# Decode attention block with gated MLP on one core: the loads of x move to GpSimd's queue, the query weights come first on ScalarE's, and ten tiny loads of x are added to SP's

## Chip, cores and metric

The kernel runs on one core of a Trainium2 chip. The metric is the device time of one launch in microseconds (us), as the median of several runs. Before the change it is 193.39 us (three runs, 193.19 to 193.43).

## What is computed

One token x of 512 bf16 numbers passes a layer norm. The result goes through attention over 32 heads with a cached window of 4096 keys and values of 128 numbers each, and beside it through a small MLP whose output gates the attention's.

```python
xn = _layernorm(x)
W = min(4096, max(256, Sk // 4))                    # 4096 of 32768
q = (xn @ wq).reshape(1, 1, 32, 128).transpose(0, 2, 1, 3)
k, v = k_cache[:, :, Sk - W:, :], v_cache[:, :, Sk - W:, :]
p = softmax(einsum("bhqd,bhkd->bhqk", q, k) * 128 ** -0.5)
s = einsum("bhqk,bhkd->bhqd", p, v).transpose(0, 2, 1, 3).reshape(1, 1, 4096) @ wo
hs = concat(shifted quarters of gelu(_layernorm(xn) @ w1)) @ w2   # one token: all quarters are zero
x1 = xn + hs
g = silu(x1 + gelu(_layernorm(x1) @ w3) @ w4)
return x + s * g
```

The two caches' windows are 33.6 MB each, wq and wo 4.2 MB each, w2, w3 and w4 together 3.3 MB. The profile counts 79.02 MB moved.

## The kernel before

**Tiling.** The 32 heads go in eight groups of four (G = 4). A group's keys are one tile K0 to K7 of 128 partitions by 128 rows by 128 numbers (4096 KB), its values one tile V0 to V7 of the same size. VectorE (DVE) works out the scores of the first 64 or 80 rows of a K tile in four parts, each a product with the query (L321) and a sum (L323); TensorE (PE) turns the other rows (L339), ScalarE (ACT) copies them out of PSUM (L342) and TensorE makes their scores (L350). The exponentials are ScalarE's (L388), the products with V TensorE's (L427). Values run two groups behind keys (LAG = 2).

**Buffers.** K tiles share three buffers (K_BUFS = 3); the first part of the output weights, wo_24, takes one of their turns between K5 and K6. V tiles share two (V_BUFS = 2). The V pool lies where the weights wq, w2, w3 and w4 lay, so V0 waits until these have landed and been used. A K or V load therefore waits for the engines to be done with the tile that had its buffer.

**The head of the kernel.** x is loaded twice, as x_bf (L79: 128 partitions, 8 bytes each) and as x_row (L82: four rows of 256 bytes), both from ScalarE's queue, ahead of the query weights wq (L84: 4096 KB, 32 KB to a partition). SP's queue issues, in this order, w2 (512 KB), w3 (1376 KB), w4 in two pieces (1280 and 96 KB), and then K0 in two halves, K0a and K0b, K1 and K2. x_bf feeds the first layer norm: L183, L160 to L178, then xn (L186, L188) and, through L194 and L196, the operand of the query product. TensorE's order is written by the scheduler: norm of x, the product of w2 with zeros (L233), L194, norm of x1, the product with w3 (a_ps, L252), and only then the 32 query products with wq (L208). The queries are spread to all partitions by L214 and L216 (q_bc), and q_bc and K0a are what the first L321 waits for. x_row is used in L242 and at the very end in L653.

**SP's queue** holds all other loads. Their order is the program's (`keep_in_program_order`), and a load that waits holds up all behind it. In each step s of the main loop (L531) K of group s is issued first (L534), then V of group s - 2 (L541, L545), then, in steps 5 and 7, parts of wo (L549, L551, L552): blocks of 2048, 1024 and 512 KB, here called wo_24, wo1 and wo2. The last V tile is issued in three pieces, V7a (2048 KB), V7b and V7c (1024 KB each), then two loads of wo_rows (256 KB each) and the output.

**Completion semaphores.** The loads issued by SP and ScalarE take eight completion semaphores in turn; the program makes a load wait until the load that had its semaphore before has landed. In what follows such a semaphore is a lane. The kernel before uses them so, each row in order of time:

| lane | loads |
|---|---|
| 0 | x_bf, K0b, K5, wo2 |
| 1 | w2, K1, V3, V6 |
| 2 | x_row, K2, wo_24, V7a |
| 3 | wq, V0, K6, V7b |
| 4 | w3, K3, V4, V7c |
| 5 | w4 (1280 KB), V1, K7, first wo_rows |
| 6 | w4 (96 KB), K4, V5, second wo_rows |
| 7 | K0a, V2, wo1, output |

So K0b waits for x_bf and K2 for x_row.

Of the kernel before, what the change touches and what calls it, by code (L numbers as in the profile page):

```python
# [8 lines left out]
P = 128  # L9
BF16 = mybir.dt.bfloat16  # L10
# [16 lines left out]
def kernel(  # L27
# [14 lines left out]
    nc = tc.nc  # L42
# [11 lines left out]
    KC = D // P  # L54
# [9 lines left out]
    small = ctx.enter_context(tc.tile_pool(name="small", bufs=1))  # L64
# [10 lines left out]
    def load(dst, src):  # L75
        return tc.keep_in_program_order(nc.sync.dma_start(out=dst, in_=src))  # L76

    x_bf = small.tile([P, KC], BF16, name="x_bf")
    nc.scalar.dma_start(out=x_bf[:], in_=A_x.rearrange("a b (p c) -> p (a b c)", p=P))  # L79
    x_row = small.tile([P, P], BF16, name="x_row")  # L80
    nc.gpsimd.memset(x_row[:], 0.0)
    nc.scalar.dma_start(out=x_row[0:P:32, :], in_=A_x.rearrange("a b (j n) -> (a b j) n", j=KC))  # L82
    wq_sb = wts.tile([P, KC, HD], BF16, name="wq_sb")
    nc.scalar.dma_start(out=wq_sb[:].rearrange("p c n -> p (c n)"),  # L84
                        in_=A_wq.rearrange("(a b c) n -> b a (c n)", a=4, c=KC))
# [5 lines left out]
    load(w4_sb[:, 0:10, :], B_w4[0:10 * P, :].rearrange("(p c) n -> p c n", p=P))  # L91
    load(w4_sb[0:96, 10, :], B_w4[10 * P:F, :])


    def load_kv(pool, cache, g, cuts=(0, CP)):
        t = pool.tile([P, CP, Dh], BF16, tag="kv", name="kv")
        src = cache[0, G * g:G * g + G, W0:, :].rearrange("a (b c) d -> b a (c d)", b=PB)
        dst = t[:].rearrange("p c d -> p (c d)")
        for c0, c1 in zip(cuts, cuts[1:]):
            load(dst[:, c0 * Dh:c1 * Dh], src[:, :, c0 * Dh:c1 * Dh])  # L100
        return t
# [115 lines left out]
    for b in range(2):  # L217
# [5 lines left out]
        for t in range(2):  # L223
            rows = slice(64 * t, 64 * t + 64)
            nc.scalar.copy(out=q_pair[rows, 4 * b:4 * b + 4, :, G * t:G * t + G].rearrange("p g l a -> p g a l"),
                           in_=qt_ps[rows].bitcast(BF16).rearrange("p g (a m l) -> p g a m l", a=G, l=2)[:, :, :, 0, :])
# [38 lines left out]
    for i in range(11):  # L265
        n = P if i < 10 else 96
# [44 lines left out]
    def k_open(g):  # L311
        st[g] = {
            "sT": ps_s.tile([P, CP - 64, G], FP32, tag="sT", name="sT"),
            "S": sm_pool.tile([P, CP], FP32, tag="S", name="S"),
        }

    def k_vector(g, kn, part):
        m = nd(g) // 4
        rows = slice(m * part, m * part + m)
        prod = prod_pool.tile([P, 20, Dh], BF16, tag="prod", name="prod")  # L320
        nc.vector.tensor_tensor(out=prod[:, 0:m, :], in0=kn[:, rows, :],  # L321
                                in1=q_bc[:, g:g + 1, :].to_broadcast([P, m, Dh]), op=ALU.mult)
        nc.vector.tensor_reduce(out=st[g]["S"][:, rows], in_=prod[:, 0:m, :], axis=AX.X, op=ALU.add)  # L323
# [3 lines left out]
    def batches(g):  # L327
        n, m = nd(g), CP - nd(g)
        k = -(-m // 8)
        edges = [n + 2 * (m // 2 * i // k) for i in range(k + 1)]  # L330
        return list(zip(edges, edges[1:]))

    def k_turn(g, kn, b):
        c0, c1 = batches(g)[b]
        n = (c1 - c0) // 2
        pt = ps_tr.tile([P, 4, P], FP32, tag="pt", name="pt")
        for i in range(n):
            c = c0 + 2 * i
            nc.tensor.transpose(pt[:, i, :], kn[:, c:c + 2, :].rearrange("p c d -> p (c d)").bitcast(FP32),  # L339
                                ident_f[:])  # L340
        kts[b] = kt_pool.tile([P, 4, 2 * P], BF16, tag="kt", name="kt")
        nc.scalar.copy(out=kts[b][:, 0:n, :], in_=pt[:, 0:n, :].bitcast(BF16))  # L342

    def k_scores(g, b):
        kt = kts.pop(b)
        c0, c1 = batches(g)[b]
        for i in range((c1 - c0) // 2):
            c = c0 + 2 * i - nd(g)
            for l in range(2):
                nc.tensor.matmul(st[g]["sT"][:, c:c + 2, :].rearrange("p c a -> p (c a)"),  # L350
                                 lhsT=kt[:, i, l::2], rhs=q_pair[:, g, l, :], start=(l == 0), stop=(l == 1))
# [55 lines left out]
    def load_wo(i):  # L407
        h0, n = blocks[i]
        load(wo_blk[i], A_wo[h0 * P:(h0 + n) * P, :].rearrange("(p t) n -> p t n", p=P))
# [4 lines left out]
    def load_rows(h, n):  # L414
        load(wo_rows[:, h - h_part:h - h_part + n, :],
             A_wo[h * P:(h + n) * P, :].rearrange("(h p) n -> p h n", p=P))
# [93 lines left out]
    def y_open():  # L510
        yr[0] = ps_tr.tile([P, KC, P], FP32, tag="pt", name="yr_ps")
        zeros(yr[0][:])
# [12 lines left out]
    NG = H // G  # L525
# [5 lines left out]
    for s in range(NG + LAG):  # L531
        h = s - LAG
        last = h == NG - 1
        kn = load_kv(k_pool, A_k_cache, s, (0, 64, CP) if s == 0 else (0, CP)) if s < NG else None  # L534
        if s == LAG:
            wts_guard.__exit__(None, None, None)
            v_pool = ctx.enter_context(tc.tile_pool(name="v", bufs=V_BUFS))
            wo_blk[2] = v_pool.tile([P, 4, D], BF16, tag="wo_4", bufs=1, name="wo_4")
            wo_rows = v_pool.tile([P, H - h_part, D], BF16, tag="wo_rows", bufs=1, name="wo_rows")
        if last:  # L540
            v = load_kv(v_pool, A_v_cache, h, cuts)  # L541
            for r in (H - G, H - 2):
                load_rows(r, 2)
        elif h >= 0:
            v = load_kv(v_pool, A_v_cache, h)  # L545
        if h == 3:
            wo_24 = k_pool.tile([P, 32, D], BF16, tag="kv", name="wo_24")
            wo_blk[0], wo_blk[1] = wo_24[:, 0:16, :], wo_24[:, 16:24, :]
            load_wo(0)  # L549
        if h == 5:  # L550
            load_wo(1)  # L551
            load_wo(2)  # L552

        if s < NG:
            nb = len(batches(s))

            def keys(b0, b1):
                for b in range(b0, b1):
                    k_turn(s, kn, b)
                    if b > 0:  # L560
                        k_scores(s, b - 1)

            k_open(s)
            k_vector(s, kn, 0)
            keys(0, 2)
            if s == 7:
                v_turn(h - 1)
                v_add(h - 1)
                v_out(h - 1)
            elif s > 1:  # L570
                sm_den(s - 2)
                sm_rden(s - 2)
            elif s == 1:
                sm_max(0)
            k_vector(s, kn, 1)
            keys(2, 4)
            if s == 7:
                sm_den(h)
                sm_rden(h)
                keys(4, nb - 2)  # L580
                sm_turn(s - 1)
                keys(nb - 2, nb)
            else:
                if s > 0:
                    sm_turn(s - 1)
                keys(4, nb)
            k_scores(s, nb - 1)
            sm_own(s)
            if s == 7:
                k_vector(s, kn, 2)  # L590
                v_wide(h, v)
                sm_exp(s - 1)
                v_turn(h)
                y_open()
                k_vector(s, kn, 3)
                v_add(h)
                v_out(h)
                ox_spread(1)
                sm_max(s)
                continue  # L600
            if s > 0:
                sm_exp(s - 1)
            if h > 0:
                v_turn(h - 1)
            k_vector(s, kn, 2)
            if h >= 0:
                v_wide(h, v)
            if h > 0:
                v_add(h - 1)
                v_out(h - 1)  # L610
            if s == 6:
                ox_spread(0)
            k_vector(s, kn, 3)
            if s == 6:
                ox_pick(0)
            if s > 0:
                sm_max(s)
        elif s == NG:
            ox_pick(1)
            sm_turn(NG - 1)  # L620
            sm_exp(NG - 1)
            y_wide(1, False)
            sm_den(NG - 2)
            sm_rden(NG - 2)
            y_wide(0, False)
            warm(3)
            v_wide(h, v)
            sm_den(NG - 1)
            sm_rden(NG - 1)
            v_turn(h)  # L630
            v_add(h)
            v_out(h)
            ox_spread(2)
        else:
            v_open(h)
            warm(3)
            v_wide(h, v, cuts[1], last=False)
            ox_pick(2)
            y_wide(2, True)
            nc.scalar.copy(out=y_sum[:], in_=yr[0][:].rearrange("p j n -> p (j n)"))  # L640
            v_wide(h, v, cuts[2], cuts[1])
            v_turn(h)
            v_add(h)
            rows_add(y_ps, ind, y_sum, False)
            v_part(h, v, cuts[2], CP)
            v_out(h)
            for r in range(H - G, H):
                y_head(r)
# [36 lines left out]
```

## Time and profile before

| | |
|---|---|
| median of three runs | 193.39 us (193.19 to 193.43) |
| span of the profiled execution, first to last instruction | 191.2 us |
| left over between the two | 2.2 us |
| DMA | 79.02 MB, mean 413 GB/s over the span |
| busy: DVE / PE / ACT / POOL | 150.9 / 116.4 / 89.2 / 2.3 us |
| x_bf: issued, landed | 0.74, 4.69 us |
| wq: issued, landed | 2.32, 19.87 us |
| K0a, K0b, K1 landed | 25.99, 32.09, 41.82 us |
| K6, V4, K7, V5 landed | 134.15, 143.80, 153.52, 163.17 us |
| wo1, wo2, V6 landed | 165.64, 166.86, 176.52 us |
| V7a, V7b, V7c, second wo_rows landed | 181.46, 183.89, 186.33, 187.61 us |

Times count from the span's start. A load has landed when its completion semaphore has received its last step, which is later than its last record. The trace also holds one record for each piece of a load that a DMA engine moved, with its queue, size and duration; q1 is SP's queue, q10 ScalarE's, q8 and q14 fetch instructions and tables. The 2.2 us between the span and the median lie outside what the profile shows.

### The profile page before, as it was taken

How to read it: one execution, taken by the hardware profiler on the slowest of the kernel's cores; microseconds unless marked ns; L12 is line 12 of the kernel's file. 1: busy time of each engine (PE TensorE's matmuls, PEld its weight loads, DVE VectorE, ACT ScalarE, POOL GpSimd, SP SyncE). 2: the span in 40 equal slices, each digit the busy share in tenths (PEclk: the TensorE clock that was granted, in tenths of full speed). 3: DMA queues.
4: the chain of work that ended last, by engine and by line, in shares of the span. 5: the costliest groups of instructions: out<-in, count | busy, mean ns of one | idle time of the engine just before them, and what ended most of it. 6: DMA issues, size and time to landing. Idle time of an engine off the chain costs nothing.

```text
span 191.2 us, 2839 instructions
## 1 busy us (share of the span) xinstructions
PE 116.4 (61%) x1159; PEld 74.2 (39%) x1159; DVE 150.9 (79%) x175; ACT 89.2 (47%) x191; POOL 2.3 (1%) x11
## 2 busy tenths in 40 slices
PE   1653754989825368256845772680888189739762
PEld 0430222767614334143334441540763077313322
DVE  1660159979999999999999999999999999980111
ACT  2001370888794076427464564542475148733120
POOL 2110000000000000000000000000000000000000
PEclk9999695555755557955695588557567858975998
DMA  6999999999999999999999999999999998999990
GB/s 211 447 430 404 431 418 439 439 439 437 432 434 439 432 429 432 432 439 432 422 432 432 418 422 418 452 439 435 439 432 434 435 432 372 471 425 405 420 371 32
DMA packets 4572, 79.02 MB, mean 413 GB/s; under 512 B 624, under 2 KB 1232, under 8 KB 1488
## 3 DMA queue, kind: packets, MB, share of 16 engines
q1 hardware_dynamic: 4264, 74.65, 91.6%
q10 hardware_dynamic: 296, 4.20, 5.1%
q8 instruction: 9, 0.15, 0.3%
q14 instruction: 3, 0.02, 0.0%
HBM read 78.84 MB, written 0.00 MB: 412 GB/s over the span
## 4 chain that ended last, share of the span: by engine, by line
DVE 46%; DMA 43%; PE 5%; ACT 3%; issue 1%; SPq 1%; ACTq 0%; DVEq 0%
DMA kv<-in_A_k_cache_dram 31%; DVE S L323 28%; DVE prod L321 15%; DMA kv<-in_A_v_cache_dram 10%; ACT kt L342 3%; DMA x_bf<-in_A_x_dram 2%; PE pt L339 2%; PE ov L427 1%; DVE m L366 1%; DVE S L364 1%; SPq L76 1%; PE sT L350 1%; DVE mx L374 1%; PE oT L461 1%; PE ot_ps L444 0%
## 5 line engine op out<-in xcount | busy, mean ns | idle before, releaser
L323 DVE TENSOR_REDUCE S<-prod 128x20 f32<-128x2560 bf16 (+1 forms) x32 | 86.0, 2686 | 1.1
L342 ACT COPY kt<-pt 128x1024 bf16<-128x1024 bf16 x52 | 51.2, 1013 | 40.4 <-PE pt L339 38.7
L339 PE MATMUL pt<-ident_f,kv 128*128 128x128 f32 x208 | 46.7, 376 | 10.8 <-DMA kv<-in_A_k_cache_dram 10.8
L321 DVE TENSOR_TENSOR prod<-kv,q_bc 128x2560 bf16<-128x2560 bf16 (+1 forms) x32 | 45.4, 1418 | 3.9 <-DMA kv<-in_A_k_cache_dram 3.7
L339 PEld LDWEIGHTS pt<-ident_f,kv 128*128 128x128 f32 x208 | 34.2, 196 | 14.4 <-DMA kv<-in_A_k_cache_dram 10.5
L350 PE MATMUL sT<-q_pair,kt 128*128 128x8 bf16 x416 | 19.4, 170 | 15.7 <-ACT kt L342 15.5
L350 PEld LDWEIGHTS <-kt 128*128 128x128 bf16 x416 | 16.4, 104 | 26.8 <-ACT kt L342 25.8
L427 PE MATMUL ov<-kv,pT 128*16 128x512 bf16 x248 | 22.0, 515 | 1.4 <-DMA kv<-in_A_v_cache_dram 1.4
L388 ACT ACTIVATE pT<-S,mb 128x128 bf16<-128x128 f32 x32 | 13.9, 573 | 0.3
L372 PE MATMUL mt_ps<-ident_f,m 128*1 128x128 f32 x8 | 2.9, 359 | 17.4 <-DVE rden L399 16.9
L433 ACT COPY ov_sb<-ov 128x512 f32<-128x512 f32 x8 | 4.7, 586 | 17.1 <-PE ov L427 17.1
L427 PEld LDWEIGHTS <-pT 128*16 128x16 bf16 x248 | 6.9, 109 | 13.2 <-issue 11.4
L359 ACT ACTIVATE own<-sT,par 128x48 f32<-128x48 f32 (+1 forms) x32 | 7.5, 356 | 3.7 <-PE sT L350 3.7
L444 PE MATMUL ot_ps<-ident_f,ov_sb 128*128 128x128 f32 x32 | 7.1, 359 | 2.9 <-ACT mb L384 1.9
L211 DVE CAST q_row<-qr_ps 128x512 bf16<-128x512 f32 x1 | 0.7, 692 | 9.9 <-PE qr_ps L208 9.9
L388 ACT ACTIVATION_READ_ACCUMULATOR pT<-S,mb 128x1 f32 x32 | 8.3, 258 | 0.0
L372 PEld LDWEIGHTS mt_ps<-ident_f,m 128*1 128x1 f32 x8 | 0.6, 80 | 17.9 <-DVE rden L399 17.2
L399 DVE RECIPROCAL rden<-den_ps 128x4 f32<-128x4 f32 x8 | 1.4, 175 | 7.0 <-PE den_ps L394 7.0
L381 PE MATMUL mb_ps<-md,par_t 5*128 5x4 f32 x16 | 3.9, 311 | 4.1 <-DVE md L376 4.1
L255 ACT ACTIVATE a_row<-a_ps 128x384 bf16<-128x384 f32 x1 | 0.5, 491 | 12.0 <-remote 12.0
L444 PEld LDWEIGHTS ot_ps<-ident_f,ov_sb 128*128 128x128 f32 x32 | 4.5, 178 | 3.9 <-ACT mb L384 2.3
L208 PE MATMUL qr_ps<-wq_sb,xq_bf 128*1 128x512 bf16 x32 | 3.1, 566 | 3.7 <-DMA wq_sb<-in_A_wq_dram 3.7
(122 smaller groups left out, 81.6 us busy)
## 6 DMA issues: line engine op xcount, KB each, us to landing
kv<-in_A_k_cache_dram SPq DMA_DIRECT2D x7, 4096.0 KB, 31.3
kv<-in_A_v_cache_dram SPq DMA_DIRECT2D x7, 4096.0 KB, 30.6
wq_sb<-in_A_wq_dram ACTq DMA_DIRECT2D x1, 4096.0 KB, 17.6
kv<-in_A_k_cache_dram SPq DMA_DIRECT2D x2, 2048.0 KB, 27.4
wo<-in_A_wo_dram SPq DMA_DIRECT2D x1, 2048.0 KB
kv<-in_A_v_cache_dram SPq DMA_DIRECT2D x1, 2048.0 KB
kv<-in_A_v_cache_dram SPq DMA_DIRECT2D x2, 1024.0 KB, 17.6
w_sb<-in_B_w_dram SPq DMA_DIRECT2D x1, 1376.0 KB, 9.1
```

The lines of the kernel that those rows point to most:

```text
L321: nc.vector.tensor_tensor(out=prod[:, 0:m, :], in0=kn[:, rows, :], in1=q_bc[:, g:g + 1, :].to_broadcast([P, m, Dh]), op=ALU.mult)
L323: nc.vector.tensor_reduce(out=st[g]["S"][:, rows], in_=prod[:, 0:m, :], axis=AX.X, op=ALU.add)
L339: nc.tensor.transpose(pt[:, i, :], kn[:, c:c + 2, :].rearrange("p c d -> p (c d)").bitcast(FP32), ident_f[:])
L342: nc.scalar.copy(out=kts[b][:, 0:n, :], in_=pt[:, 0:n, :].bitcast(BF16))
L350: nc.tensor.matmul(st[g]["sT"][:, c:c + 2, :].rearrange("p c a -> p (c a)"), lhsT=kt[:, i, l::2], rhs=q_pair[:, g, l, :], start=(l == 0), ...
L359: nc.scalar.mul(s["own"][:, 0:m, a], s["sT"][:, 0:m, a], par[:, a:a + 1])
L372: nc.tensor.transpose(mt_ps[:], s["m1"][:], ident_f[:])
L381: nc.tensor.matmul(mb_ps[:], lhsT=par_t[:].rearrange("k b a -> k (b a)"), rhs=md[:], start=True, stop=True)
L388: nc.scalar.activation(out=s["pT"][:, :, a], in_=s["S"][:], func=ACT.Exp, scale=scale, bias=mb[:, a:a + 1], accum_out=s["sum"][:, a:a + 1])
L427: nc.tensor.matmul(ov[r:r + 4 * G], lhsT=s["pT"][:, c:c + 4, :].rearrange("p i a -> p (i a)"), rhs=v[:, c:c + 4, :], start=(i < 4), stop=( ...
L433: nc.scalar.copy(out=s["ov_sb"][:], in_=ov[:])
L444: nc.tensor.transpose(ot_ps[:, step * j:step * j + P], s["ov_sb"][:, j, :], ident_f[:])
```

## The change

x_bf and x_row are issued by GpSimd, so that wq is the first load on ScalarE's queue. A small tile `marks` is added, into which SP loads ten tiny pieces of x (k rows of 32 bytes, k as listed; nothing reads them): five after K7 in step 7, and five after wo2 in the same step.

```diff
-    nc.scalar.dma_start(out=x_bf[:], in_=A_x.rearrange("a b (p c) -> p (a b c)", p=P))
+    nc.gpsimd.dma_start(out=x_bf[:], in_=A_x.rearrange("a b (p c) -> p (a b c)", p=P))
     x_row = small.tile([P, P], BF16, name="x_row")
     nc.gpsimd.memset(x_row[:], 0.0)
-    nc.scalar.dma_start(out=x_row[0:P:32, :], in_=A_x.rearrange("a b (j n) -> (a b j) n", j=KC))
+    nc.gpsimd.dma_start(out=x_row[0:P:32, :], in_=A_x.rearrange("a b (j n) -> (a b j) n", j=KC))
...
+    marks = small.tile([16, 16, 16], BF16, name="marks")
+
+    def mark(ks):
+        for k in ks:
+            load(marks[0:k, k, :], A_x[0, 0, 0:16 * k].rearrange("(k n) -> k n", k=k))
...
         kn = load_kv(k_pool, A_k_cache, s, (0, 64, CP) if s == 0 else (0, CP)) if s < NG else None
+        if s == NG - 1:
+            mark((1, 3, 5, 7, 2))
...
             load_wo(1)
             load_wo(2)
+            mark((9, 11, 13, 15, 14))
```

In the built program this moves more than the diff shows. GpSimd's loads have semaphores of their own, so the lanes of all later loads turn. The marks are called m1, m3 and so on by their k:

| lane | loads after the change |
|---|---|
| 0 | wq, K2, wo_24, m2, m14 |
| 1 | w2, V0, K6, V5, V6 |
| 2 | w3, K3, V4, wo1, V7a |
| 3 | w4 (1280 KB), V1, K7, wo2, V7b |
| 4 | w4 (96 KB), K4, m1, m9, V7c |
| 5 | K0a, V2, m3, m11, first wo_rows |
| 6 | K0b, K5, m5, m13, second wo_rows |
| 7 | K1, V3, m7, m15, output |

K0b and K1 no longer wait for a lane; K2 waits for wq; V5 waits for K6, wo1 for V4, wo2 for K7, and V6 for V5. GpSimd's order becomes: x_bf, the memsets of x_row and ident_bf, x_row, ident_bf's select, ident_f's memset, the power of the first norm (L178 before), and only then ident_f's select. On VectorE only the reduction that makes `ind` (L120 before) moves, two places later. TensorE's and ScalarE's orders are otherwise the same.

## Prediction

> **What bounds the kernel.** I read the DMA rows of the page first, then the chain, then what SP's queue waits for, then the timeline at the three places that the change touches: the head, the stretch from 130 to 168 us, and the tail.
>
> ```profile
> DMA  6999999999999999999999999999999998999990
> q1 hardware_dynamic: 4264, 74.65, 91.6%
> q10 hardware_dynamic: 296, 4.20, 5.1%
> q8 instruction: 9, 0.15, 0.3%
> DVE 46%; DMA 43%; PE 5%; ACT 3%; issue 1%; SPq 1%; ACTq 0%; DVEq 0%
> ```
>
> The queues' shares add to 97.0% of the span: 185.5 us on each of 16 engines. By the trace's records the first byte of a load moves at 1.74 us and the last load lands at 187.61, a stretch of 185.9 us. So the DMA engines have at most some 0.4 us without a record in the whole kernel. The bound is the sum of the records' durations; an earlier load gains only by starting the stream earlier, and a later one loses only by letting it run dry. The chain names DVE for 46%, since K buffers become free by DVE; but a buffer that comes free late costs nothing while other loads are queued. At 130.25 us, when K7 is issued, the engines are still at K6, landing at 134.15, and then V4, until 143.80: 13.5 us of stock. For V7a, issued at 166.55 with V6 landing at 176.52, it is 10.0 us.
>
> DVE is nearly a second bound, though:
>
> ```profile
> DVE prod L321 <- DMA kv<-in_A_k_cache_dram: 1.5, 2, 1.0
> DVE mx L374 <- PE mt_ps L372: 0.5, 2, 0.4
> ```
>
> These are all of DVE's waits from 41.9 to 172 us: 2.0 us, 1.0 of it ahead of K1 at 41.91. A delay that DVE has at 42 us is carried to the tail almost whole. And in the tail TensorE works just behind the landings:
>
> ```profile
> 181.50 1.04 PE L427 MATMUL ov<-kv,pT 128*16 128x512 bf16 x16 [1.02 <-DMA kv<-in_A_v_cache_dram]
> ...
> 183.93 0.61 PE L427 MATMUL ov<-kv,pT 128*16 128x512 bf16 x8 [0.41 <-DMA kv<-in_A_v_cache_dram]
> ...
> 186.38 0.96 PE L461 MATMUL oT<-pT,kv 128*128 128x4 bf16 x32 [0.17 <-DMA kv<-in_A_v_cache_dram]
> ```
>
> It waits 1.02 + 0.41 + 0.17 = 1.6 us for the three pieces of V7.
>
> **Part 1: wq first, SP's waits on x gone.** SP waits for x like this:
>
> ```profile
> SPq L76 <- DMA x_bf<-in_A_x_dram: 1.4, 1, 1.4
> SPq L76 <- DMA x_row<-in_A_x_dram: 0.9, 1, 0.9
> ```
>
> K0b and K2 are thereby issued at 4.71 and 6.83 us, while the engines have w2, w3, w4, wq and K0a to move until 26 us. Taking 2.3 us of such waiting away starts no byte earlier: gain 0. The new wait of K2 for wq holds it to some 14 us, with K0b and K1 (landed at 32.09 and 41.82) queued ahead of it: cost 0. The stream's start is w2's, issued at 0.73 us, and stays.
>
> What changes is the order in which the head's bytes come. In the records the two queues take turns piece by piece: x_bf's 8-byte records (9 ns) alternate one for one with w2's of 4096 bytes (159 ns), and later wq's eight records to an engine of 32 KB (1213 ns) with w3's of 11,008 (413 ns) and others. In the kernel before ScalarE's first records came at 2.35 us; wq, now first, takes its turns from there. Six of w2's eight are then left: 6 x (1.213 + 0.159) = 8.2, so w2 ends near 10.6 us (it landed at 4.52). The last two of wq alternate with w3: 2 x 1.63 = 3.3, so wq ends near 13.9 instead of 19.87, and w3, with six records left, near 16.4 instead of 10.32. The sum of bytes ahead of K0a is the same, so K0a still lands at 26.0.
>
> TensorE's order makes w3 count: a_ps (2.9 us, from 13.25 to 16.17) stands ahead of the query product, so it now starts near 16.5 and the query product near 19.4 instead of 19.91, when it waited for wq. Half a us earlier buys nothing, for DVE's first product waits for K0a:
>
> ```profile
> 26.09 1.23 DVE L321 TENSOR_TENSOR prod<-kv,q_bc 128x2048 bf16<-128x2048 bf16 x1 [2.19 <-DMA kv<-in_A_k_cache_dram]
> ```
>
> **Part 2: x through GpSimd.** No load of GpSimd's is in this trace. The row nearest to it is the same load from ScalarE, 0.74 to 4.69: 3.95 us. That is the low end. The high end is that GpSimd's records take turns singly as ScalarE's did, now against 32 KB records of wq in each round: eight rounds of 1.37 to 1.63 us from about 3 us on, so x_bf lands about when wq does, near 14.2 us.
>
> What x may cost is worked out back from K0a. From x's landing to z_bf is 13.20 - 4.69 = 8.5 us, a_ps 2.9, and from the query product to the first q_bc 24.02 - 19.91 = 4.1: x + 15.5 us, against 26.0. Up to x at 10.5 us nothing moves; with the 1.0 us that DVE waits ahead of K1, up to 11.5. I take the near row with a us or so on top, x at 5 to 6 us: cost 0. GpSimd's own order costs nothing either: ident_f's select (0.29 us) now follows the power (7.50 to 8.05), and `ind`, its first reader, was moved behind on DVE.
>
> The Trainium skill (DMA: Bandwidth & Descriptors, "Queues, rings and completion order" and "SWDGE vs HWDGE vs iDMA") says that an engine drains a whole packet of one ring before it turns to the next, and that GpSimd's descriptors are put into packets of up to 64. By that rule x_bf's eight pieces on an engine would need one turn, not eight, and x would land near the low end. The turns of single 8-byte records in this trace are of ScalarE's queue and neither bear it out nor speak against it.
>
> **Part 3: the ten marks.** As transfers: a mark is at most one data record and one semaphore record on an engine. Records of 8 bytes took 9 ns and of 256 bytes 15 to 18, semaphores 9, so a mark costs an engine 18 to 27 ns, and ten at most 0.27 us, if they all fall on the engine that ends last; nothing if they fall on others (the engines' last steps for V6 came between 174.60 and 176.52, so 15 of them have slack). I take 0.1.
>
> As issues on SP and by their lanes:
>
> ```profile
> 130.25 0.54 SPq L76 DMA_DIRECT2D kv<-in_A_k_cache_dram  x1
> 130.88 1.30 SPq L76 DMA_DIRECT2D kv<-in_A_v_cache_dram  x1
> 132.22 1.06 SPq L76 DMA_DIRECT2D wo<-in_A_wo_dram  x2
> 148.33 20.06 SPq L76 DMA_DIRECT2D kv<-in_A_v_cache_dram  x4
> ```
>
> After K7 at 130.25 come five marks, 0.4 to 0.55 us each as SP's other issues; the lanes that m7 and m2 wait for (V3, wo_24) had landed at 119.52 and 124.43. V5 waits for K6 and goes out at 134.2 instead of 130.88, with V4 and K7 queued until 153.5. wo1 waits for V4: 143.8. wo2 waits for K7: 153.5, with V5 queued until 163.17. The next five marks go out by 156. Then **V6 waits for V5**: 163.2 instead of 148.33. Queued behind V5 are then only wo1 and wo2, which end on the slowest engine at 166.86, 3.7 us on, and on the fastest at 164.95. From an issue to its first record w2 took 1.74 - 0.73 = 1.0 us, so V6's records come from 164.3: in time on all engines, with 0.6 us to spare on the fastest and 2.5 on the slowest. V7a waits for wo1 (165.64) and, as before, for TensorE (166.55); V7b for wo2 (166.86, it went out at 167.15); V7c and the rest for marks just behind wo2. Their stock is V6's 9.7 us. So the cover is thin in one place, and holds. TensorE needs V5 at 164.60, after it landed; V5, wo1, wo2 and V6 keep their places in the stream. Cost 0.
>
> **Sum.** The profiled execution: 191.2 us of span and 2.2 outside. Head 0, x 0, waits 0, marks +0.1: 191.3 and 2.2, or 193.5 us against the median of 193.39.
>
> **The rivals.**
> - **x lands late (slower).** With x at 14.2 us DVE starts K1 2.7 us late. It gets back the 0.55 us that it waits for K6 and up to 0.36 at L374, so it enters the tail some 2 us late; TensorE's 1.6 us of waits absorb most, but not all in one order (y_wide and the warm-ups stand between). I put the end 0.7 us later, 194.1; between 2.7 - 0.9 - 1.6 = 0.2 and, if only the wait of 1.02 us counts, 1.7. It decides from x at 11.5 us on. For it: the records' one-by-one turns. Against: the near row of 3.95 us, and x's issue at the same instant as wq's, whose queue gave its first record only at 2.35.
> - **V6 runs dry (slower).** If an issue takes longer than 3.7 us to its first record behind a deep queue, the slowest engine stands still; with 3.95 us, a small load's whole time, by 0.3 us, and the skew of 1.9 us between engines may add to it: 193.8 to 194.5. Against: w2's 1.0 us.
> - **A cheaper head (faster).** w2's 4096-byte records in the cold head took up to 849 ns; all 256 of that size took 198 ns in the mean against a usual 159, which is 0.6 us to an engine. If wq's large records, coming first, bear the start better, up to 0.6 us of it comes back: 192.9. Against: the slow records are the first of the stream, whatever they carry.
> - **The change does nothing where it matters:** that is my forecast.
>
> The Trainium skill (DMA: Bandwidth & Descriptors, "Issuing engines are not separate DMA queues") says the same of the head: loads from several engines run on the same 16 DMA engines and interleave, so another issuer saves only issue time. The trace agrees: SP's and ScalarE's records alternate on the same engines and the total rate stays near 430 GB/s.
>
> **How the numbers follow.** 0.2% of the time is 0.39 us, about what a measurement can tell from no change. Forecast (x before 11.5 us, V6 in time): 0.57. x late 0.24, V6 dry 0.07, cheaper head 0.12. Of the forecast's 0.57 I give 0.02 to more than 0.2% slower. The late x mostly ends past 193.78 us, but a fifth of it within: so slower 0.28, same 0.60, faster 0.12. The range runs from 192.9, the cheap head, to 194.6, within the late x.
>
> **What would show it.** Right: x_bf landing before 11 us, L321's first product at 26.1 with a wait for K0a, K1's first product at 41.9; wq landing near 14 and w3 near 16.5; V6 issued near 163.2 and landing at 176.5; V7c landing at 186.3. Wrong: a first product that starts when q_bc is written, DVE without waits at K1 and K6, or a slice near 164 us in which the DMA row drops below 9.

## The result, and the profile after

The changed kernel takes 194.29 us (median of 17 runs, 193.74 to 195.2), the kernel before on the same chip 193.41 (17 runs, 193.14 to 194.07): a ratio of 1.0047, interval 1.0036 to 1.0059. That is 0.9 us slower, where 0.1 us was forecast. The time lies within the range; the likeliest case, no difference that can be measured, did not come, and the range held by luck: it went up to 194.6 for an x that lands too late to be free, which did not happen.

The profiled execution took 193.82 us with a span of 191.7, so 2.1 us lie outside of it, as before (2.2): the loss is inside the span. The page's DMA rows and its chain, in the order in which they were shown of before:

```profile
DMA  6999999999999999999999999999999999999990
q1 hardware_dynamic: 4424, 74.65, 91.4%
q10 hardware_dynamic: 144, 4.19, 5.1%
q0 software_dynamic: 64, 0.00, 0.0%
DVE 46%; DMA 41%; PE 6%; ACT 3%; SPq 2%; issue 1%; ACTq 0%; DVEq 0%
```

q0 is GpSimd's queue, new here: 64 records without a visible share. The marks are 160 more records on q1. The row of tenths shows nothing; the loss is smaller than a slice can tell. Two of DVE's waits between 41 and 175 us (us in total, times, the longest), those that the prediction showed of before, are the same to 0.2 us, so nothing that x's detour did at the head has reached the main loop by way of DVE:

```profile
DVE prod L327 <- DMA kv<-in_A_k_cache_dram: 1.6, 2, 1.1
DVE mx L380 <- PE mt_ps L378: 0.6, 1, 0.6
```

At the head, the timeline has the cast that waits for x_bf, and the first product, which waits for K0a as before:

```profile
8.95 0.17 DVE L189 CAST x_f<-x_bf 128x4 f32<-128x4 bf16 x1 [7.61 <-DMA x_bf<-in_A_x_dram]
...
25.82 1.22 DVE L327 TENSOR_TENSOR prod<-kv,q_bc 128x2048 bf16<-128x2048 bf16 x1 [2.41 <-DMA kv<-in_A_k_cache_dram]
```

x_bf is 4.2 us later than before and this costs the first product nothing: it starts at 25.82, 0.27 us earlier than before, since K0a landed at 25.72 instead of 25.99. Up to wo2 the whole stream is 0.2 us ahead of before (K1 41.62, V5 162.97, wo2 166.68). Then it loses. SP's issues in that stretch (start, us to the next, with a wait inside where it is long):

```profile
130.64 1.74 SPq L76 DMA_DIRECT2D marks<-in_A_x_dram  x5
...
134.01 0.54 SPq L76 DMA_DIRECT2D kv<-in_A_v_cache_dram  x1
143.62 10.06 SPq L76 DMA_DIRECT2D wo<-in_A_wo_dram  x2
153.72 1.92 SPq L76 DMA_DIRECT2D marks<-in_A_x_dram  x5
163.04 6.92 SPq L76 DMA_DIRECT2D kv<-in_A_v_cache_dram  x4
```

V6 goes out at 163.04, when V5 has landed, 14.7 us later than before. One line for the stretch from 163 to 172 us (busy times of the engines, then TensorE's clock, DMA share, GB/s) of the kernel before and of the one after:

```profile
163.00:172.00 9.00, 4.62 (x60) 2.44 (x59) 8.21 (x13) 4.64 (x16) 0.00 (x0) 0.85 1.04 444
```

```profile
163.00:172.00 9.00, 5.89 (x59) 2.55 (x58) 8.31 (x13) 4.64 (x16) 0.00 (x0) 0.77 1.02 421
```

The last column is the finding: 23 GB/s less over 9 us are 0.21 MB, or 0.5 us at 444 GB/s, while the share of busy time hardly falls. Most of the loss is records that take longer; the table behind e4_twelve has them. The tail is late by what is left of this, with TensorE still just behind the landings:

```profile
181.92 1.04 PE L433 MATMUL ov<-kv,pT 128*16 128x512 bf16 x16 [0.45 <-DMA kv<-in_A_v_cache_dram]
...
184.35 0.61 PE L433 MATMUL ov<-kv,pT 128*16 128x512 bf16 x8 [0.40 <-DMA kv<-in_A_v_cache_dram]
...
186.80 0.96 PE L467 MATMUL oT<-pT,kv 128*128 128x4 bf16 x32 [0.17 <-DMA kv<-in_A_v_cache_dram]
```

Each starts 0.42 us later than before. This profile explains +0.4 us; the median is +0.9. The 17 times also reach higher than those of before: six lie from 194.65 to 195.2.

### The profile page after: what moved, and what is told of

It is laid out like the page before. It is cut to its first block, busy times and chain, and to the rows that moved or that the text cites. A ratio compares the mean times of both kernels' runs of the same rounds, so it can differ in the third digit from the quotient of the medians.

```text
span 191.7 us, 2850 instructions
## 1 busy us (share of the span) xinstructions
PE 115.2 (60%) x1159; PEld 73.1 (38%) x1159; DVE 151.0 (79%) x175; ACT 88.8 (46%) x191; POOL 3.7 (2%) x13
## 4 chain that ended last, share of the span: by engine, by line
DVE 46%; DMA 41%; PE 6%; ACT 3%; SPq 2%; issue 1%; ACTq 0%; DVEq 0%
DMA kv<-in_A_k_cache_dram 32%; DVE S L329 28%; DVE prod L327 15%; DMA kv<-in_A_v_cache_dram 9%; ACT kt L348 3%; SPq L76 2%; PE ov L433 2%; PE pt L345 2%; PE sT L356 1%; DVE m L372 1%; DVE S L370 1%; DVE mx L380 1%; PE oT L467 1%; PE ot_ps L450 0%; DVE md L382 0%
## 5 line engine op out<-in xcount | busy, mean ns | idle before, releaser
L345 PE MATMUL pt<-ident_f,kv 128*128 128x128 f32 x208 | 44.6, 363 | 10.5 <-DMA kv<-in_A_k_cache_dram 10.5
L345 PEld LDWEIGHTS pt<-ident_f,kv 128*128 128x128 f32 x208 | 32.9, 189 | 13.8 <-DMA kv<-in_A_k_cache_dram 10.1
L433 PE MATMUL ov<-kv,pT 128*16 128x512 bf16 x248 | 23.7, 547 | 0.8 <-DMA kv<-in_A_v_cache_dram 0.8
L387 PEld LDWEIGHTS mb_ps<-md,par_t 5*128 5x128 f32 x16 | 3.4, 260 | 6.5 <-PE sT L356 5.0
```

Source lines behind the costliest of these rows:

```text
L387: nc.tensor.matmul(mb_ps[:], lhsT=par_t[:].rearrange("k b a -> k (b a)"), rhs=md[:], start=True, stop=True)
L433: nc.tensor.matmul(ov[r:r + 4 * G], lhsT=s["pT"][:, c:c + 4, :].rearrange("p i a -> p (i a)"), rhs=v[:, c:c + 4, :], start=(i < 4), stop=( ...
```

## The experiments

For the marks, theory R: with V6 issued only when V5 has landed, SP's queue is nearly empty when V6 arrives, and filling it again costs. For the head, the question came with the first runs: some executions take 1 us more. Theory S lays this to GpSimd's loads of x, W to the order with wq first, F to a fetch of instructions that meets an engine already behind.

**e1_head**: the loads of x and the order of the head as changed, no marks.

```diff
-    marks = small.tile([16, 16, 16], BF16, name="marks")
...
-            mark((1, 3, 5, 7, 2))
...
-            mark((9, 11, 13, 15, 14))
```

> The head of the change alone: x by GpSimd, wq first, no marks; V6 waits for nothing of the late loads, as in the kernel before. Theory R (refill: the loss comes from V6 being issued only when V5 has landed, 163.0 us instead of 148.3, so that the faster engines' first V6 records took 1.3 to 1.9 us instead of 1.213): as before, 193.2 to 193.5 us, V6 issued near 148, its last record steps near 176.3, V7c landed near 186.1. Theory H (head: x landing at 8.9 us and the other order of wq and w3 cost the time): 194.3. Theory M (each mark costs the stream some 0.09 us as a transfer): 193.4.

Measured: 194.25 us against 193.42 of the kernel before, ratio 1.0036 (1.0019 to 1.0053). The 12 runs fall into two groups: five from 193.39 to 193.73 and seven from 194.09 to 194.85. The profiled one is of the lower group (193.39) and lies within 0.2 us of before at the landings of K0a, K1, V6, the pieces of V7 and the second wo_rows.

**e2_marks**: the marks alone; x comes from ScalarE, ahead of wq, as before.

```diff
-    nc.gpsimd.dma_start(out=x_bf[:], in_=A_x...)
+    nc.scalar.dma_start(out=x_bf[:], in_=A_x...)
...
-    nc.gpsimd.dma_start(out=x_row[0:P:32, :], in_=A_x...)
+    nc.scalar.dma_start(out=x_row[0:P:32, :], in_=A_x...)
```

> The ten marks alone, x on ScalarE as before. The lanes turn by two against the change, and every late load waits for the same load as in the change: V5 for K6, wo1 for V4, wo2 for K7, V6 for V5. Theory R: as the change, 194.0 to 194.6, V6 issued near 163.2 and slow first V6 records. Theory H: 193.4. Theory M: 194.3 too, so this run tells H from the others, not R from M.

Measured: 194.14 us, ratio 1.0026 (1.0014 to 1.0038), 11 runs from 193.71 to 194.32. Against the median of before they are late by 0.3 to 0.9 us, 0.7 in the median. Its line for 163 to 172 us shows the 421 GB/s of after again:

```profile
163.00:172.00 9.00, 5.14 (x71) 2.89 (x69) 8.66 (x13) 5.31 (x16) 0.00 (x0) 0.99 1.04 421
```

**e3_nine**: the whole change without m14, so that V6's lane is m2's.

```diff
-            mark((9, 11, 13, 15, 14))
+            mark((9, 11, 13, 15))
```

> The change with one mark less (m14 left out): V6's semaphore is then that of m2, landed at 153 us, so V6 goes out near 155.5 with 8 us of stock ahead; V7a waits for V5, V7b for wo1, V7c for wo2, all landed before these are issued. Theory R: the whole loss goes, 193.2 to 193.6. Theory M: nine tenths of it stays, 194.2. Theory H: 194.3.

Measured: 193.56 us, ratio 1.0013 (0.9997 to 1.0029): nine runs from 193.28 to 193.72, three at 194.18, 194.62 and 194.71. SP's issue of V6 and the stretch:

```profile
155.52 14.50 SPq L76 DMA_DIRECT2D kv<-in_A_v_cache_dram  x4
```

```profile
163.00:172.00 9.00, 5.94 (x59) 2.49 (x57) 8.42 (x13) 4.75 (x16) 0.00 (x0) 0.77 1.05 443
```

Nine marks and 7.5 us more of head start, and the stretch is that of before. As transfers the marks cost nothing that shows: the lower groups of e3_nine and e1_head have the same median, 193.5.

**e4_twelve**: two marks more (k = 10 and 12), so that V6 waits for wo2, the last load ahead of it.

```diff
-            mark((9, 11, 13, 15, 14))
+            mark((9, 11, 13, 15, 14, 10, 12))
```

> The change with two marks more (k = 10 and 12) behind m14: V6 then waits for wo2, landed at 166.7, and is issued near 166.8 instead of 163.0, when every engine has moved all that was queued. Theory R: first V6 records near 168.2 on all engines, which the faster ones started at 165.4 before the change; V6 ends near 178.5 on them instead of 174.5 and the end moves by as much: 196.5 to 197.8. Theory M: 194.5. Theory H: 194.3.

Measured: 197.38 us, ratio 1.0201 (1.018 to 1.0221). V6 is issued at 166.60, its first record starts at 167.94, and TensorE waits at V7's first piece:

```profile
166.60 3.10 SPq L76 DMA_DIRECT2D kv<-in_A_v_cache_dram  x4
```

```profile
180.54 3.51 PE L433 MATMUL ov<-kv,pT 128*16 128x512 bf16 x32 [3.79 <-DMA kv<-in_A_v_cache_dram]
```

**R is borne out**: issued at 155.5, V6 costs nothing; at 163.1, 0.7 us; at 166.6, 4.0 us (this one with GpSimd's x_bf, which may hold a part of it). The trace's records tell what kind of loss it is. These are the records of 32 KB that start between 163.9 and 170 us, all of them V6's. The last column counts the time from 164 to 172 us in which an engine had no record at all, the 16 engines added up; it is found by counting the records that are open at each moment, which are never fewer than 16 in this stretch before the change:

| kernel | V6 issued | first record | over 1300 ns | longest, ns | time over 1213 ns, mean of an engine | without a record, us, 16 engines |
|---|---|---|---|---|---|---|
| before | 148.33 | 164.49 | 0 | 1213 | 0 | 0 |
| e3_nine | 155.52 | 164.43 | 2 | 1361 | 21 ns | 0 |
| after | 163.04 | 164.50 | 12 | 1904 | 246 ns | 1.2 |
| e2_marks | 163.07 | 164.56 | 15 | 2080 | 401 ns | 0.7 |
| e4_twelve | 166.60 | 167.94 | 12 | 2086 | 355 ns | 47.1 |

After the change V6's first record starts when it did before. But the first records of the refilled queue take up to 1904 ns instead of 1213, and up to two of the 16 engines stand still between 164.4 and 165.2 us: 1.2 us in all, against 3.9 us in long records. In e4_twelve the first engine stands still from 164.3 us, and all of them from the end of wo2's records (166.1) to 167.9.

**e5_both**: for the head. The kernel before, with its two loads of x on ScalarE kept (nothing reads them) and x loaded by GpSimd as well.

```diff
+    nc.gpsimd.dma_start(out=x_bf[:], in_=A_x...)
+    x_bf2 = small.tile([P, KC], BF16, name="x_bf2")
-    nc.scalar.dma_start(out=x_bf[:], in_=A_x...)
+    nc.scalar.dma_start(out=x_bf2[:], in_=A_x...)
...
+    nc.gpsimd.dma_start(out=x_row[0:P:32, :], in_=A_x...)
+    x_row2 = small.tile([P, P], BF16, name="x_row2")
-    nc.scalar.dma_start(out=x_row[0:P:32, :], in_=A_x...)
+    nc.scalar.dma_start(out=x_row2[0:P:32, :], in_=A_x...)
```

> No marks. ScalarE's loads stay as before the change (two copies of x that nothing reads, then wq), and GpSimd loads the x that is used. It leaves V6, the lanes and the order of wq and w2 as before. It is meant for the extra 1 us that some executions with wq first and x on GpSimd take (e1_head: about half of them at 194.1 to 194.9, the others at 193.4 to 193.7). Theory S, GpSimd's loads (a late x in some executions) bring it: some executions here at 194.1 or more, median 193.6 or more. Theory W, the order with wq first brings it: all executions at 193.0 to 193.9, median within 0.2 us of the kernel before. Theory F, it falls on any kernel in which an instruction fetch meets the engine that is behind: as theory W here, since the stream is that of before.

Measured: 195.39 us against 193.57, ratio 1.0092 (1.0078 to 1.0106), all four runs from 195.07 to 195.49. The first product starts 1.09 us later than before, with a wait for K0a, so it is the stream that is late and not x:

```profile
27.18 1.23 DVE L325 TENSOR_TENSOR prod<-kv,q_bc 128x2048 bf16<-128x2048 bf16 x1 [3.61 <-DMA kv<-in_A_k_cache_dram]
```

Neither W nor F is needed for the delay: the order of ScalarE's and SP's loads is that of before, and the delay is there at 27 us, ahead of the first 16 KB fetch (27.58). S holds, but 1.8 us is more than the 1 us that it was to explain. The rest came from the experiment itself: the two unread tiles shift later tiles by 264 bytes, and the records of V0 to V6 took 1216 ns in the median instead of 1213, those of K3 to K5 1218.

**e6_sp**: wq first on ScalarE, x_bf and x_row from SP ahead of w2, nothing from GpSimd.

```diff
-    nc.scalar.dma_start(out=x_bf[:], in_=A_x...)
+    load(x_bf[:], A_x...)
...
-    nc.scalar.dma_start(out=x_row[0:P:32, :], in_=A_x...)
+    load(x_row[0:P:32, :], A_x...)
```

> No marks. wq is ScalarE's first load, as after the change, but x_bf and x_row are loaded by SP ahead of w2, so GpSimd loads nothing. w2 is issued some 1 us later; wq's records may start the stream in its place at 2.4 to 3.6 us, so the stream and the end may move by 0 to 0.7 us in all executions alike. Theory W, the order with wq first brings the extra 1 us in some executions: two groups about 1 us apart, as in e1_head. Theory S, GpSimd's loads bring it: one group, with all executions within 0.6 us of each other, median 193.3 to 194.1.

Measured: 194.03 us, ratio 1.0024 (1.0009 to 1.0039), 12 runs spread from 193.39 to 195.47. It answers neither theory. Without w2 in front, wq's own records open the stream, and 37 of them took over 1230 ns in the profiled execution (up to 2324 for 1213); K0a landed at 26.78, 0.8 us later than before. So it has a cost of its own. This execution is the slowest of the twelve (195.47), and 1.2 of its 2.1 us of extra span come behind the second wo_rows' landing: TensorE starts V6's product at 179.87 us instead of 176.56. Why it starts late stays open.

**e1_look2 and e1_look3**: the kernel e1_head, profiled twice more.

> The same kernel as e1_head, profiled again to catch an execution of its upper group. A single time either at 193.4 to 193.7 or at 194.1 to 194.9. In an upper one: theory S expects x_bf landing at 11.5 us or later and a first product later than 25.8; theory W expects x_bf near 9.0 and K0a landing later than 25.7, so that the 1 us is there by K1's landing (41.6); theory F expects the head as in e1_head's first profile and the loss later, at an engine that has had a fetch record of about 1.05 us.

> As the look before it: the same kernel as e1_head once more, a single time either at 193.4 to 193.7 or at 194.1 to 194.9, with the same three expectations of an upper one (S: x_bf at 11.5 us or later; W: K0a and K1 late by about 1 us; F: head unchanged, loss later at an engine with a fetch record).

They came out at 193.31 and 194.32 us, one of each group. The cast of x_bf and the first product, of the one and of the other:

```profile
8.85 0.17 DVE L183 CAST x_f<-x_bf 128x4 f32<-128x4 bf16 x1 [7.51 <-DMA x_bf<-in_A_x_dram]
...
25.82 1.23 DVE L321 TENSOR_TENSOR prod<-kv,q_bc 128x2048 bf16<-128x2048 bf16 x1 [2.74 <-DMA kv<-in_A_k_cache_dram]
```

```profile
9.71 0.17 DVE L183 CAST x_f<-x_bf 128x4 f32<-128x4 bf16 x1 [8.37 <-DMA x_bf<-in_A_x_dram]
...
26.69 1.23 DVE L321 TENSOR_TENSOR prod<-kv,q_bc 128x2048 bf16<-128x2048 bf16 x1 [2.82 <-DMA kv<-in_A_k_cache_dram]
```

The second one, of the upper group, is 0.86 us late from x_bf on, again with a wait for K0a. The trace has x_bf as one record of 64 bytes on each engine, at about 6.5 us. Their durations in ns, in order of size:

```
e1_look2    15 x13   25  138  151
e1_look3    15 x8    51  241  448  460  684  734  865  865
e5_both     15 x5   104  138  144  256  256  265  289  341  351  444  716
after, e1_head, e3_nine, e4_twelve    15 x16 each
```

Two engines lose 0.85 us with a 64-byte record. K0a lands when the last engine has landed it, and this is 26.59 us instead of 25.72: the 0.87 us are there. That these two engines are the last is inferred, since the trace doesn't name the engine of a record. From K0a to the second wo_rows both executions take 161.64 us. The expectation had this wrong in one point: S looked for x at 11.5 us or later and a late x as the price. x was late by 0.9 us only; the price is the engines that it held up.

**e7_pad**: e5_both with 512 bytes of unread tiles instead of 264.

```diff
-    x_bf2 = small.tile([P, KC], BF16, name="x_bf2")
+    x_bf2 = small.tile([P, P], BF16, name="x_bf2")
```

> The kernel e5_both, with its unread copy of x_bf in a tile of 256 bytes, so that the two copies together move later tiles by 512 bytes and not by 264. In e5_both the records of V0 to V6 took 1216 ns where they take 1213 before, besides K0a landing 1.09 us late (27.08 against 25.99). If the address of the tiles did the first, these records are back at 1213 here and the end gains 0.3 to 0.5 us. Theory S (GpSimd's 64-byte records of x_bf, 15 to 716 ns each there, put single engines back): K0a still at 26.3 to 27.1 and a median of 194.0 to 195.0. Rival A (the address did all of it): K0a at 26.0 and a median of 193.3 to 193.7.

Measured: 194.41 us, ratio 1.0048 (1.003 to 1.0066). K0a landed at 26.84, the records of V0 to V6 are back at 1213 ns, and from K0a to the second wo_rows it takes 161.63 us (e5_both 162.42, before 161.62). So GpSimd's loads cost about 1 us at the head, and the 264 bytes 0.8 us later on, more than the 0.3 to 0.5 expected. Here the 64-byte records took at most 318 ns, less than K0a lost (0.85 us). The rest shows as engines without a record: up to ten of the 16 stand still at once between 5.5 and 6.6 us, around x_bf's records, 5.4 us in all. e5_both loses 5.5 us there too, the kernel before and e1_look3 0.1 or less. So x_bf's records cost in two ways, as long records and as gaps around them.

**e8_row**: the kernel before and a further load of x_row by GpSimd, unread.

```diff
+    x_row2 = small.tile([P, 2, P], BF16, name="x_row2")
+    nc.gpsimd.dma_start(out=x_row2[0:P:32, 0, :], in_=A_x...)
```

> The kernel before, and one more load of x_row by GpSimd that nothing reads (four pieces of 256 bytes; its tile takes 512 bytes). In all profiles so far GpSimd's 256-byte records took 18 ns and only its 64-byte records of x_bf were slow in some. Theory S: no loss, median 193.3 to 193.7, K0a at 26.0. Rival G (any load of GpSimd's costs the stream, by its descriptors or its queue, whatever its records take): K0a at 26.3 or later and a median of 194.0 or more.

Measured: 193.52 us against 193.44, ratio 1.0006 (0.9994 to 1.0017); K0a at 25.98. x_row's load by GpSimd shows no cost, so it is not any load of GpSimd's; x_bf's shape on GpSimd's queue is what costs.

**e9_late**: the kernel before and four further loads of x_bf by GpSimd, unread, once the weights' place is free (issued at 32.04 to 33.82 us).

```diff
+        if s == LAG + 2:
+            for i in range(4):
+                x_bf2 = v_pool.tile([P, KC], BF16, tag=f"x_bf2{i}", bufs=1, name="x_bf2")
+                nc.gpsimd.dma_start(out=x_bf2[:], in_=A_x...)
```

> The kernel before, and four more loads of x_bf by GpSimd that nothing reads, issued when the weights' place is free, near 31 us, so that they meet the stream of 32 KB records and not its start. If the slow 64-byte records belong to the first microseconds (like w2's first records of 4096 bytes, up to 849 ns instead of 159): all 64 of them take about 15 ns, median 193.2 to 193.8. If they belong to GpSimd's loads of this shape whenever they come: some of 100 to 865 ns again, and with four loads a median of 194.3 to 196.

Measured: 194.51 us, ratio 1.0057 (1.0038 to 1.0077), four runs from 194.23 to 195.16. The profiled execution is the slowest (195.16). Its K0a landed at 26.30, so 0.3 us were lost ahead of these loads; from K0a to the second wo_rows it takes 162.30 us, 0.7 more than before. Thirteen of the 64 records took over 30 ns, the longest 376, K1's records beside them 1255 ns in the mean instead of 1217, and engines stood still for 5.7 us in all between 36 and 42 us, where the kernel before has no such gap. The cost doesn't belong to the first microseconds.

**e10_repair**: the change with both costs taken out: nine marks, and x_bf from ScalarE ahead of wq. x_row stays on GpSimd.

```diff
-    nc.gpsimd.dma_start(out=x_bf[:], in_=A_x...)
+    nc.scalar.dma_start(out=x_bf[:], in_=A_x...)
...
-            mark((9, 11, 13, 15, 14))
+            mark((9, 11, 13, 15))
```

> The change with its two costs taken out as the runs so far have them: nine marks instead of ten, so that V6 waits for m2 and not for V5, and x_bf from ScalarE ahead of wq, while x_row stays on GpSimd. If the refill (0.7 us) and GpSimd's x_bf (0 or 1 us) are all that the change costs: one group at 193.2 to 193.8, median within 0.2 us of the kernel before. If x_row on GpSimd or the marks themselves cost something as well: some executions at 194.1 or more, or a median over 193.8.

Measured: 193.51 us, 12 runs from 193.29 to 193.83, ratio 1.0003 (0.9995 to 1.0012). One group, at the time of the kernel before, so the two costs are all that the change has, to the 0.2 us that the interval leaves. With x_bf back on ScalarE, wq is no longer first, and this run doesn't tell these two apart; that x_bf by GpSimd costs with the old order too, e5_both and e7_pad show. No kernel here beats the one before.

All profiled executions side by side, from the trace's landings. The first column tells what the head costs, the last what comes behind it, to the last load:

| kernel | K0a landed | second wo_rows landed | between |
|---|---|---|---|
| before | 25.99 | 187.61 | 161.62 |
| e1_look2 | 25.72 | 187.36 | 161.64 |
| e1_look3 | 26.59 | 188.23 | 161.64 |
| e7_pad | 26.84 | 188.47 | 161.63 |
| e10_repair | 25.98 | 187.70 | 161.72 |
| e1_head | 25.84 | 187.52 | 161.68 |
| e8_row | 25.98 | 187.54 | 161.56 |
| e6_sp | 26.78 | 188.48 | 161.70 |
| e5_both | 27.08 | 189.50 | 162.42 |
| e9_late | 26.30 | 188.60 | 162.30 |
| e3_nine | 25.89 | 187.69 | 161.80 |
| after | 25.72 | 188.02 | 162.30 |
| e2_marks | 25.74 | 188.27 | 162.53 |
| e4_twelve | 25.68 | 191.48 | 165.80 |

## Why the prediction was right and wrong, step by step

**The bound** was right: the stream's time is the sum of the records' durations, engine by engine, and both costs are longer records, with gaps beside some of them. What the prediction held constant was the duration of a record of a given size.

**Part 1** was right in its cost of 0, with landings that were off. SP waits 12.6 us for wq ahead of K2, as foreseen, and nothing is late by it:

```profile
SPq L76 <- DMA wq_sb<-in_A_wq_dram: 12.6, 1, 12.6
```

wq landed at 17.45 instead of the forecast 13.9, and w2 at 4.45 instead of 10.6, since wq's records began at 3.6 us and not at 2.35: all but nine of w2's 128 records had started by then. The first product waited for K0a as forecast.

**Part 2** named the right price for the wrong thing. x_bf landed at 8.93, beyond the 5 to 6 us that were taken and well within the 10.5 up to which it is free. That one 64-byte record serves an engine's eight pieces agrees with the rule of the Trainium skill that the prediction weighed (DMA: Bandwidth & Descriptors, "SWDGE vs HWDGE vs iDMA"): x_bf needed one turn. x_bf did not land near the low end all the same, since its first record came 5.3 us after the issue (1.24 to 6.53), and ScalarE's 1.6 us (0.74 to 2.35). The cost, 0 in some executions and about 1 us in others, was in no term of the sum: the prediction asked only when x arrives, not what its records do to the engines that carry it. Why they are long, or have gaps around them, in some executions stays open. Size alone is not it. The same page of the Trainium skill says that transfers below 512 bytes need a read-modify-write ("Specifications"); but x_row's 256-byte records took 18 ns from GpSimd in every profile, and ScalarE's 8-byte records of x_bf 7 to 9 ns. Whether wq ahead of x adds to it was not settled either: e6_sp was the attempt.

**Part 3** holds the step that failed: **"V6's records come from 164.3: in time on all engines, with 0.6 us to spare on the fastest and 2.5 on the slowest"**, and with it "Cost 0". The first of them came at 164.50, 1.46 us behind the issue and not 1.0, and not in time on all engines: up to two stood still from 164.4 to 165.2. The 0.6 us to spare were not there. They were counted to wo2's first landing step, 164.95, but the fastest engine was through with wo2 earlier: before, its first record of V6 began at 164.49. So the term for V6's wait is 0.7 us (e2_marks against before) and not 0. It is made of these gaps (less than 0.1 us on the mean engine) and, for the most part, of the first records of a refilled queue, which are longer: a quarter to 0.4 us on the mean engine.

The sentence beside it failed as well, that 15 engines "have slack". By the records of 4 bytes that close V6, seven of the sixteen ended it at 174.9 to 175.1 instead of 174.2 to 174.6, while the last ended no later than before. By records that follow each other without a gap (an inference; the trace doesn't name the engine), one of the seven then carried a fetch of 16 KB for the instructions (884 ns at 176.33), and the record behind it took 1158 ns instead of 611. It became the last to end V7a, at 181.39. The slack of that engine had been spoken for already before: there, too, one of the seven had the fetch (1019 ns at 175.26, then a record of 1115) and ended V7a at 181.02, level with the engine that ended V6 last. In e2_marks V6 itself landed late, at 177.15 instead of 176.52. The marks as transfers were forecast at 0.1 us and cost nothing that shows.

**The sum.** 0.7 us for V6 and 0 or about 1 us for x_bf, which fits six of the 17 runs at least, go with the +0.9 us of the median. The rival "V6 runs dry" had the right place and, with 193.8 to 194.5, the right time, but got 0.07. Its reason, engines that stand still, is the smaller part of the loss after the change (1.2 of some 5 us, the 16 engines added up) and the larger one only in e4_twelve. "x lands late" had about the right time, 194.1, for the wrong reason: x landed early enough. The measured time is in the range because this rival set its upper end; both terms that were paid stood in the sum as 0.

**What would show it** was partly blind: V6's issue, the first product and K1 (41.71) were as forecast for "right", V7c landed 0.4 us late, and the DMA row near 164 us stays at 9 although the loss is there (before, the slice ahead of it had an 8). GB/s over the stretch shows it.

## What to carry to other kernels

A stream of DMAs loses before it stops: a load that must wait until its queue is nearly drained can have its first record in time and still cost, so judge a wait by what is queued behind the load it waits for (here an issue 8.9 us ahead of the first record was free, one of 1.5 us was not), and read GB/s over the stretch and the records' lengths, not the busy share. Count such a margin to the last record of the fastest engine, not to a landing step. Where every byte is on the path, a small load is priced by what its records hold up on the slowest engine, not by its bytes or its landing. An engine that ends early in one place may have a fetch waiting in the next.

## What the runs showed of the hardware that was not expected

- The first records behind a nearly empty queue are long: up to 2080 ns for 32 KB against 1213 in midstream; at the start of the kernel before, w2's of 4096 bytes took up to 849 ns against 159.
- x_bf by GpSimd goes as one 64-byte record to an engine, all of 15 ns in four of the eight profiled executions that load it at the head, up to 151, 318, 716 and 865 in the others, with up to ten engines without a record beside them in e7_pad; by ScalarE as eight of 8 bytes, 7 to 9 ns each.
- Fetches of instructions show as nine records of 16 KB and about 1 us in each profile, and the stream pays more than that. A data record that starts within 16 ns of a fetch's end is long in every profile, all but the last fetch having one: 1674 to 1775 ns for 32 KB instead of 1213, 1076 to 1158 for 16 KB instead of 611. So a fetch costs its engine about 1.5 us.
- A shift of later tiles by 264 bytes lengthened V's 32 KB records from 1213 to 1216 ns and the stretch from K0a to the end by 0.8 us; 512 bytes did neither. Which tile's address it is was not tried.
